# Two feed-forward units moved into the last expert slot, and the weight splits spread over fifteen units

## The chip, the cores and the metric

The kernel runs on one core of a Trainium2 chip. The metric is the device time of one execution, in microseconds (us). Engines are named as the profile names them: PE (TensorE, matrix products), DVE (VectorE), ACT (ScalarE), POOL (GpSimd) and SP (SyncE, which here only issues DMAs). Each engine works through its own instructions in order; semaphores make one engine wait for another.

## The reference

Three layers over 2304 tokens of width 512, all in float32:

```
scores = mask(q @ k.T / 8); attn = softmax(scores) @ v        # 4 x 8 heads, 576 tokens, blocks of 64
e = argmax(xn @ en.T / tau); x = gate * (relu(x @ w1[e]) @ w2[e])   # 8 experts, 512 -> 1024 -> 512
h = x @ w_in                                                   # feed-forward: 512 -> 2048
g = (a0 + a1 h + a2 h^2 + a3 h^3) / (1 + |b0||h| + |b1| h^2 + 1e-6)
out = g @ w_out                                                # 2048 -> 512
```

The change concerns the last layer and its border with the experts.

## The kernel before, in words

Attention comes first, then the experts, then the feed-forward layer. The experts work on slots of 128 tokens that go to the same expert: 23 slots here, and a conditional block (`tc.If(live > COMMON)`, L1219) would do further ones; in these runs it is skipped, but every engine has to reach it and step over it. A slot gathers its tokens, turns them (L783), multiplies by w1 (L816), applies relu (L824), turns the result (L831; L839 and L840 copy it to SBUF, L845 makes its remainder), multiplies by w2 (L861), scales by the gate (ACT, `ys`, L874) and scatters to `x2_d` (POOL, L875). HEAD, PLAN1 and FOOT are strings that write out the order of these steps; FOOT has the last slots, 20 to 22.

Products keep float32 accuracy by splitting every operand into a rounded part and a remainder: `hi` is a copy rounded to the PE's format, `lo` is the operand minus `hi`, and a product is three matmuls (hi x hi, hi x lo, lo x hi).

The feed-forward layer has 96 **units**: six token blocks J of 384 tokens, times 16 slices f of 128 hidden columns. A unit has 12 matmuls into a PSUM tile `mp` (`hidden`, L1273), a chain of elementwise steps that forms g, and 9 matmuls that add g @ w_out to three accumulators (`project`, L1349). The chain, by the letters that the plan string UNIT uses: S, A, U (ACT: the square, |b0 h| and a2 + a3 h, L1283 to L1291), q (DVE: the denominator, L1303), d and e (DVE: the numerator, L1295 and L1299, the last readers of `mp`), R and Q (ACT: reciprocal root and its square, L1307 and L1312), E (DVE, L1316), r (ACT, L1320), f (DVE, L1324), g (DVE, L1328), h (DVE: `gh`, the rounded g, L1332) and l (POOL: `gl`, the remainder, L1337). R needs another table on ACT than the steps ahead of it, so the first R is led by a table load.

UNIT interleaves units: a letter with a digit n in period t works on unit t - n. So in period t PE does the products of unit t (H0) and then the projection of unit t - 3 (P3); DVE does E of unit t - 1, h of t - 2, q and d of t, f of t - 1, e of t and g of t - 1. `mp` has two buffers, so H of unit t waits for step e of unit t - 2.

Weights of the feed-forward layer arrive coded and are decoded during the expert phase. The tiles of the first PRE = 4 slices f are split there at once (hi on ACT, L217, lo on POOL, L218) and kept; the other 24 are stored to `w_d` and come back during the first feed-forward units (`load_w`, L1249; four staging tiles `wst`). There `split_w` makes hi (L1261, on DVE) and lo (L1264, DVE and POOL by turns). Period t of the first 20 uses the plan FIRST, with two such splits each.

At the end `deliver` copies the three accumulators to SBUF (L1364, L1366) and POOL sends them (L1372).

Of the kernel before, what the change touches and what calls it, by code (L numbers as in the profile page):

```python
# [29 lines left out]
PRE = 4  # L30
# [17 lines left out]
FOOT = "C00.20 C01.20 L10.19 D C02.20 T0.19 L11.19 R10.20 T1.19 AH.19 C03.20 AL0.19 G.22 X.21 XH.21 XL.21 H00.21 C10.19 L00.21 C11.19 D C12.19 C13.19 R11.20 H01.21 L02.21 RL.20 L01.21 R00.22 L03.21 D R01.22 T0.20 D H10.20 Y.19 L10.20 L11.20 T1.20 C00.21 C01.21 R10.21 D C02.21 AH.20 AL0.20 X.22 XH.22 C03.21 H00.22 L01.22 C10.20 L00.22 XL.22 C11.20 H01.22 RL.21 C12.20 C13.20 R11.21 D L02.22 H10.21 C00.22 L03.22 C01.22 T0.21 L11.21 D L10.21 Y.20 T1.21 AH.21 AL0.21 R10.22 D C02.22 C03.22 C10.21 C11.21 C12.21 RL.22 C13.21 R11.22 T0.22 H10.22 Y.21 D L10.22 L11.22 T1.22 AH.22 D AL0.22 D C10.22 C11.22 C12.22 D D C13.22 Y.22 D"  # L48
# [7 lines left out]
def block_attn_moe_moe2(ctx: ExitStack, tc, ap):  # L56
# [1169 lines left out]
    with ExitStack() as c3:  # L1226
        wt_b = c3.enter_context(tc.tile_pool(name="wt_b", bufs=1, side="right"))
        st_p = c3.enter_context(tc.tile_pool(name="st", bufs=NST))
        x2_p.append(c3.enter_context(tc.tile_pool(name="x2b", bufs=1)))
        g_p = c3.enter_context(tc.tile_pool(name="g", bufs=2))  # L1230
        ps_a = c3.enter_context(tc.tile_pool(name="ps_a", bufs=NA, space=PSUM))
# [35 lines left out]
        def hidden(i):  # L1267
            J, f = seq[i]
            xh, xl = x2_t[J]
            hp = ps_m.tile([128, TN], F32, name="mp", tag="mp")  # L1270
            for k in range(4):
                for n, (ww, xx) in enumerate(((wih, xh), (wil, xh), (wih, xl))):
                    nc.tensor.matmul(  # L1273
                        out=hp, lhsT=ww[f][:, k], rhs=xx[:, k], start=(k == 0 and n == 0), stop=(k == 3 and n == 2))
            if f == 15:
# [3 lines left out]
        def h_sq(i):
            hp, y, sq, t, q, g = e_t[i]
            nc.scalar.activation(out=sq, in_=hp, func=ACTF.Square)  # L1283

        def h_abs(i):
            hp, y, sq, t, q, g = e_t[i]
            nc.scalar.activation(out=q, in_=hp, func=ACTF.Abs, scale=ab[:, 4:5])  # L1287

        def h_top(i):
            hp, y, sq, t, q, g = e_t[i]  # L1290
            nc.scalar.activation(out=t, in_=hp, func=ACTF.Identity, scale=ab[:, 3:4], bias=ab[:, 2:3])  # L1291

        def p_two(i):
            hp, y, sq, t, q, g = e_t[i]
            nc.vector.tensor_tensor(out=t, in0=t, in1=hp, op=ALU.mult)  # L1295
# [12 lines left out]

        def q_inv(i):
            hp, y, sq, t, q, g = e_t[i]  # L1310
            y = e_t[i][1] = ps_z.tile([128, TN], F32, name="zp", tag="zp")
            nc.scalar.activation(out=y, in_=g, func=ACTF.Square)  # L1312

        def q_err(i):
            hp, y, sq, t, q, g = e_t[i]
            nc.vector.scalar_tensor_tensor(out=q, in0=q, scalar=ONE6, in1=y, op0=ALU.add, op1=ALU.mult)  # L1316

        def e_sq(i):
            hp, y, sq, t, q, g = e_t[i]
            nc.scalar.activation(out=q, in_=q, func=ACTF.Square, scale=-1.0, bias=three2)  # L1320

        def y_fix(i):
            hp, y, sq, t, q, g = e_t[i]
            nc.vector.scalar_tensor_tensor(out=y, in0=q, scalar=0.75, in1=y, op0=ALU.add, op1=ALU.mult)  # L1324

        def g_mul(i):
            hp, y, sq, t, q, g = e_t[i]
            nc.vector.scalar_tensor_tensor(out=g, in0=t, scalar=ab[:, 0:1], in1=y, op0=ALU.add, op1=ALU.mult)  # L1328

        def g_hi(i):  # L1330
            g_t[i] = [g_p.tile([128, TN], F32R, name=n, tag=n, bufs=NG) for n in ("gh", "gl")]
            nc.vector.tensor_copy(g_t[i][0], e_t[i][5])  # L1332

        def g_lo(i):
            gh, gl = g_t[i]
            eng = nc.vector if i == len(seq) - 1 else nc.gpsimd
            eng.tensor_tensor(out=gl, in0=e_t.pop(i)[5], in1=gh.bitcast(F32), op=ALU.subtract)  # L1337

        def project(i):
# [5 lines left out]
            if i == len(seq) - 1:  # L1345
                parts = [(t, n) for ns in ((0, 1), (2,)) for t in range(3) for n in ns]
# [34 lines left out]
        def next_x2(i):  # L1381
# [65 lines left out]
```

## Time and profile before

| what | us |
|---|---|
| median of 3 runs (lowest, highest) | 991.58 (984.66, 993.79) |
| the profiled execution | 985.55 |
| its span, first to last instruction | 983.5 |
| busy in the span: PE, DVE, ACT, POOL | 926.5, 790.2, 684.6, 288.4 |
| mean granted PE clock | 0.987 of full speed |

The profiled execution is 6.03 us under the median of the runs and 2.05 us longer than its own span. Times in rows count from the start of the span. A busy PE hides every other engine, so the places to look at are those where PE is idle or its granted clock is below 1. The feed-forward layer begins at 546.55 us.

### The profile page before, as it was taken

To read this page: it belongs to the slowest core of one execution; us is meant where nothing else is said; L and a number is where in the kernel's file an instruction comes from. 1 tells how busy PE (TensorE), PEld (TensorE's weight loads), DVE (VectorE), ACT (ScalarE), POOL (GpSimd) and SP (SyncE) were. 2 spreads that over 40 slices of the span, in tenths; PEclk is the share of its full clock that TensorE was granted. 3 is DMA by queue.
4 is the path that set the end of the run, shared out by engine and by line. 5 is a ranking of instruction groups with operands and counts; after the bars stand their busy time and mean duration, and the time that the engine had idled before them with its cause. 6 is when DMAs were issued, how large, how long until landed. Compare 5 with 4: busy or idle time off the path is not lost. (4 is left out here: it accounts for less than half of the span.)

```text
span 983.5 us, 15433 instructions
## 1 busy us (share of the span) xinstructions
PE 926.5 (94%) x5120; PEld 740.1 (75%) x5120; DVE 790.2 (80%) x1484; ACT 684.6 (70%) x1380; POOL 288.4 (29%) x266
## 2 busy tenths in 40 slices
PE   6999999879889999999999788999999999999995
PEld 5777777664566777777776576889999999999994
DVE  5778788846687786988874599898988898988884
ACT  6777878653665676877765566777777777777773
POOL 4333333201112211333321255232232322322322
PEclk9999999989999999999999999999999999999998
DMA  8227161821267458557324342000101001000000
GB/s 254 70 91 218 59 203 50 299 69 44 79 214 255 177 192 295 172 205 251 129 77 149 108 132 61 33 33 1 35 31 33 22 12 33 33 1 1 33 1 32
DMA packets 43984, 103.00 MB, mean 105 GB/s; under 512 B 6006, under 2 KB 7158, under 8 KB 43904
## 3 DMA queue, kind: packets, MB, share of 16 engines
q1 hardware_dynamic: 38784, 86.54, 27.0%
q0 software_dynamic: 5120, 15.47, 4.4%
q8 instruction: 41, 0.67, 0.3%
q14 instruction: 39, 0.32, 0.1%
HBM read 140.27 MB, written 21.76 MB: 165 GB/s over the span
## 5 line engine op out<-in xcount | busy, mean ns | idle before, releaser
L1337 POOL TENSOR_TENSOR gl<-g,gh 128x384 fp32r<-128x384 f32 x95 | 106.0, 1116 | 247.1 <-DVE gh L1332 218.2
L1273 PE MATMUL mp<-x2h,wih 128*128 128x384 f32 x384 | 130.0, 338 | 5.9 <-DVE t L1299 4.8
L1273 PE MATMUL mp<-x2l,wih 128*128 128x384 f32 x384 | 130.0, 339 | 0.0
L1273 PE MATMUL mp<-x2h,wil 128*128 128x384 f32 x384 | 129.3, 337 | 0.0
L1349 PE MATMUL acc<-woh,gl 128*128 128x512 f32 x288 | 114.9, 400 | 5.9 <-POOL gl L1337 5.9
L769 DVE TENSOR_TENSOR wl<-w0r,wh 128x1024 fp32r<-128x1024 f32 x84 | 98.9, 1221 | 23.8 <-ACT wh L763 22.7
L1349 PE MATMUL acc<-woh,gh 128*128 128x512 f32 x288 | 115.0, 399 | 0.1
L1349 PE MATMUL acc<-wol,gh 128*128 128x512 f32 x288 | 113.7, 395 | 0.0
L1303 DVE SCALAR_TENSOR_TENSOR q<-sq,absb,q 128x384 f32<-128x384 f32 x96 | 83.5, 869 | 31.2 <-ACT q L1287 30.7
L816 PE MATMUL hp<-wh,x 128*128 128x512 f32 x336 | 103.8, 431 | 0.2 <-ACT wh L763 0.2
L1283 ACT ACTIVATE sq<-mp 128x384 f32<-128x384 f32 x96 | 47.0, 489 | 78.5 <-PE mp L1273 75.7
L763 ACT ACTIVATE wh<-w0r 128x2048 fp32r<-128x2048 f32 x42 | 79.5, 1909 | 9.8 <-DMA w0r<-in_moe_w 7.4
L342 ACT ACTIVATE p<-s,nm 128x128 f32<-128x128 f32 (+2 forms) x144 | 78.4, 555 | 11.4 <-DVE nm L355 6.2
L875 POOL DMA_INDIRECT x_d<-ys,sct_i x23 | 35.3, 1537 | 167.5 <-ACT ys L874 155.6
L861 PE MATMUL yp<-w1r,hf 128*128 128x512 f32 x184 | 83.4, 592 | 0.0
L393 ACT ACTIVATE pt<-tp 128x128 f32<-128x128 f32 (+2 forms) x144 | 54.2, 423 | 39.7 <-PE tp L431 26.2
L1273 PEld LDWEIGHTS mp<-x2h,wih 128*128 128x128 f32 x384 | 72.3, 188 | 11.6 <-DVE t L1299 5.9
L816 PEld LDWEIGHTS hp<-wh,x 128*128 128x128 f32 x336 | 61.2, 192 | 19.2 <-issue 8.9
L1273 PEld LDWEIGHTS mp<-x2h,wil 128*128 128x128 f32 x384 | 72.3, 188 | 3.8
L1273 PEld LDWEIGHTS mp<-x2l,wih 128*128 128x128 f32 x384 | 72.3, 188 | 0.0
L1349 PEld LDWEIGHTS acc<-woh,gl 128*128 128x128 f32 x288 | 54.1, 188 | 22.6 <-POOL gl L1337 11.3
L1307 ACT ACTIVATE g<-q,one 128x384 f32<-128x384 f32 x96 | 59.5, 620 | 16.3 <-DVE q L1303 15.4
(304 smaller groups left out, 2252.7 us busy)
## 6 DMA issues: line engine op xcount, KB each, us to landing
w0r<-in_moe_w SPq DMA_DIRECT2D x44, 1024.0 KB
w1r<-in_moe_w SPq DMA_DIRECT2D x44, 1024.0 KB
w<-in_moe_w_in SPq DMA_DIRECT2D x16, 512.0 KB
w<-in_moe_w_out SPq DMA_DIRECT2D x16, 512.0 KB
w_d<-dm SPq DMA_DIRECT2D x24, 256.0 KB
wst<-w_d SPq DMA_DIRECT2D x24, 256.0 KB
kr<-in_k SPq DMA_DIRECT2D x16, 288.0 KB
xr<-x_d SPq DMA_DIRECT2D x6, 768.0 KB
```

Of the source, the lines that this page charges most:

```text
L342: nc.scalar.activation(out=pt, in_=src, func=ACTF.Exp, bias=bi, accum_out=pair_t[n][3][:, c, hh:hh + 1])
L393: nc.scalar.activation(out=o, in_=i, func=ACTF.Copy)
L763: nc.scalar.activation(out=out, in_=src, func=ACTF.Copy)
L769: eng.tensor_tensor(out=wl, in0=w_raw[m][k][:, j], in1=wh_t[s, m, k][:, j].bitcast(F32), op=ALU.subtract)
L816: nc.tensor.matmul(out=hp[:, n], lhsT=xx[:, ks], rhs=ww[:, 512 * n:512 * n + 512], start=(c == 0 and j == 0), stop=(c == 3 and j == len(pa ...
L861: nc.tensor.matmul(out=yp, lhsT=xx[:, 128 * f:128 * f + 128], rhs=ww[:, 512 * j:512 * j + 512], start=(c == 0 and q == 0 and j == 0), stop ...
L1273: nc.tensor.matmul(out=hp, lhsT=ww[f][:, k], rhs=xx[:, k], start=(k == 0 and n == 0), stop=(k == 3 and n == 2))
L1283: nc.scalar.activation(out=sq, in_=hp, func=ACTF.Square)
L1303: nc.vector.scalar_tensor_tensor(out=q, in0=sq, scalar=absb[:, 1:2], in1=q, op0=ALU.mult, op1=ALU.add)
L1307: nc.scalar.activation(out=g, in_=q, func=ACTF.Abs_reciprocal_sqrt, bias=one6)
L1337: eng.tensor_tensor(out=gl, in0=e_t.pop(i)[5], in1=gh.bitcast(F32), op=ALU.subtract)
L1349: nc.tensor.matmul(out=acc[J][t], lhsT=gg[:, 128 * t:128 * t + 128], rhs=ww[f], start=(f == 0 and n == 0), stop=(f == 15 and n == 2))
```

## The change

- The first HOIST = 2 units (all steps but the projection) run in FOOT, inside slot 22, ahead of the conditional block. Their products go to PSUM tiles of the expert pools, and their chains work in the staging tile of w1 (`w_raw`), which slot 22 has used up by then; gh and gl go to a pool of their own (`gx`).
- PRE is 5: ten decoded tiles are split and kept in the expert phase, not eight. 22 tiles remain to be brought back.
- The splits are spread over periods 2 to 16, one in even and two in odd periods. hi is made on ACT instead of DVE; lo of a w_in tile is made on DVE, lo of a w_out tile on POOL. LATE = 4 orders a slice's w_out tile four places behind its w_in tile.
- One plan serves all periods; the splits stand at its end (i0 behind Q0, o0 behind g1).
- The pools of the feed-forward layer wait for the tiles whose memory they reuse (`reuse_waits="tile"`), not for the pools as wholes.
- The last unit's nine projection matmuls finish the accumulators one by one.

```diff
-PRE = 4
+PRE = 5
...
-LATE = 2
-ON = 20
+LATE = 4
+HOIST = 2
+SPLITS = range(2, 17)
...
-HI = 'vvv'
-LO = 'vp'
...
-FIRST = 'H0 i0 O0 S0 E1 A0 h2 q0 U0 r1 X0 P3 d0 R0 f1 o0 e0 Q0 l2 g1 i0 o0'
-UNIT = 'H0 s1 O0 S0 E1 A0 h2 q0 U0 r1 X0 P3 d0 R0 f1 e0 Q0 l2 g1'
-LAST = UNIT
+UNIT = 'H0 s1 O0 S0 E1 A0 h2 q0 U0 r1 X0 P3 d0 R0 f1 e0 Q0 i0 l2 g1 o0'
...
+    def h_tile(i):
+        if i == 0:
+            return pool["ps_x"].tile([128, 512], F32, name="xp", tag="xp")[:, 0:TN]
+        if i < HOIST:
+            return pool["ps_h"].tile([128, 2, 512], F32, name="hp", tag="hp")[:, 0, 0:TN]
+        return ff["m"].tile([128, TN], F32, name="mp", tag="mp")
...
+        if i < HOIST:
+            raw = w_raw[0][i].rearrange("p a f -> p (a f)")
+            e_t[i] = [hp, raw[:, 4 * TN:5 * TN]] + [raw[:, TN * n:TN * n + TN] for n in range(4)]
...
-        ps_m = c3.enter_context(tc.tile_pool(name="ps_m", bufs=NM, space=PSUM))
+        ff["m"] = c3.enter_context(tc.tile_pool(name="ps_m", bufs=NM, space=PSUM, reuse_waits="tile"))
...
             if kind == "i":
-                if HI[n % len(HI)] == "a":
-                    nc.scalar.activation(out=hi, in_=st_t[n], func=ACTF.Copy)
-                else:
-                    nc.vector.tensor_copy(hi, st_t[n])
+                nc.scalar.activation(out=hi, in_=st_t[n], func=ACTF.Copy)
             else:
-                eng = nc.gpsimd if LO[n % len(LO)] == "p" else nc.vector
+                eng = nc.vector if late[n] < 16 else nc.gpsimd
...
-                parts = [(t, n) for ns in ((0, 1), (2,)) for t in range(3) for n in ns]
+                parts = [(0, 0), (0, 1), (1, 0), (0, 2), (1, 1), (1, 2), (2, 0), (2, 1), (2, 2)]
...
-        due = dict.fromkeys(unit, 0)
+        due = dict.fromkeys(unit, HOIST)
+        due["P"] = 0
...
-            t = 0
+            t = HOIST
...
-                        split_w(name)
+                        for _ in range((1 + t % 2) * (t in SPLITS)):
+                            split_w(name)
```

The FOOT string of the change is that of before with the hoisted steps written in, as `uH.0` for step H of unit 0. What this makes of ACT's order inside slot 22 shows in two pieces, first before, from the last relu to the conditional block (`wh` and `ys` are the slot's weight copy and output, `hh` and `hf` its turned relu):

```order
L824 ACTIVATE hs<-hp 128x1024
L763 ACTIVATE wh<-w1r_144 128x2048
L874 ACTIVATE ys<-yp,gate_s 128x512
L839 ACTIVATE hh<-tp 128x512
L840 ACTIVATE hf<-tp 128x512
L874 ACTIVATE ys<-yp,gate_s 128x512
L1218 TENSOR_LOAD enc_i
```

And the same place in the change (`w0r_142` and `w0r_143` are the scratch of units 0 and 1):

```order
L871 ACTIVATE ys<-yp,gate_s 128x512
L1144 ACTIVATE w0r_142<-xp 128x384
L1148 ACTIVATE w0r_142<-xp,ab 128x384
L1152 ACTIVATE w0r_142<-xp,ab 128x384
L836 ACTIVATE hh<-tp 128x512
L837 ACTIVATE hf<-tp 128x512
L1168 ACT_TABLE_LOAD
...
L1174 ACTIVATE w0r_143<-w0r_143 128x384
L1182 ACTIVATE w0r_143<-w0r_143,three_105 128x384
L871 ACTIVATE ys<-yp,gate_s 128x512
```

Unit 0's first three steps now stand ahead of slot 22's `hh`, and the slot's last `ys` stands behind step r of unit 1.

The second place is DVE in one of the first feed-forward periods. Before, from E to E:

```order
L1316 SCALAR_TENSOR_TENSOR q<-q,zp 128x384
L1332 CAST gh<-g 128x384
L1303 SCALAR_TENSOR_TENSOR q<-sq,absb,q 128x384
L1295 TENSOR_TENSOR t<-t,mp 128x384
L1324 SCALAR_TENSOR_TENSOR zp<-q,zp 128x384
L1264 TENSOR_TENSOR wil_6209<-wst,wih_6208 128x512
L1299 SCALAR_TENSOR_TENSOR t<-t,ab,mp 128x384
L1328 SCALAR_TENSOR_TENSOR g<-t,ab,zp 128x384
L1261 CAST woh_6202<-wst 128x512
L1261 CAST wih_6212<-wst 128x512
```

In the change:

```order
L1178 SCALAR_TENSOR_TENSOR q<-q,zp 128x384
L1196 CAST gh<-g 128x384
L1164 SCALAR_TENSOR_TENSOR q<-sq,absb,q 128x384
L1156 TENSOR_TENSOR t<-t,mp 128x384
L1186 SCALAR_TENSOR_TENSOR zp<-q,zp 128x384
L1160 SCALAR_TENSOR_TENSOR t<-t,ab,mp 128x384
L1190 SCALAR_TENSOR_TENSOR g<-t,ab,zp 128x384
L1355 TENSOR_TENSOR wil_6280<-wst,wih_6279 128x512
```

The two casts have left DVE, and the one subtraction has moved behind g.

## Rows read from the trace of the kernel before

**Rows 1.** The page's first line.

```profile
span 983.5 us, 15433 instructions
```

**Rows 2.** Windows: stretch, length, then busy us (instructions) of PE, PEld, DVE, ACT, POOL; clock, DMA.

```profile
553.75:559.30 5.55, 3.49 (x18) 3.17 (x19) 5.55 (x12) 4.14 (x8) 1.54 (x2) 1.00 0.47 119
559.30:562.70 3.40, 3.40 (x11) 2.62 (x10) 3.40 (x8) 2.05 (x5) 2.40 (x2) 0.52 0.39 119
562.70:620.00 57.30, 50.99 (x245) 41.91 (x244) 57.23 (x113) 36.56 (x72) 27.57 (x21) 1.00 0.31 88
620.00:960.00 340.00, 340.00 (x1728) 307.80 (x1728) 299.80 (x581) 256.73 (x506) 103.47 (x95) 1.00 0.06 22
```

**Rows 3.** The chain that ended last: start, us, what; PE's pieces in the steady stretch.

```profile
616.86 2.11 PE mp L1273 x12
618.96 0.33 PE zp L1111 x3
619.29 2.08 PE acc L1349 x9
```

**Rows 4.** Timeline, border of experts and feed-forward: start, us, engine, line, [idle before <-releaser].

```profile
536.10 1.04 PE L831 MATMUL tp<-ident,hs 128*128 128x128 f32 x8
539.40 0.74 PE L861 MATMUL yp<-wh,hl 128*128 128x512 f32 x2 [0.85 <-DVE hl L845]
545.53 0.69 ACT L874 ACTIVATE ys<-yp,gate_s 128x512 f32<-128x512 f32 x1 [7.28 <-PE yp L861]
546.53 26.84 SPq L1249 DMA_DIRECT2D wst<-w_d  x13
546.55 0.44 PE L1273 MATMUL mp<-x2h,wih 128*128 128x384 f32 x1 [1.06 <-ACTq L1219]
...
550.61 1.28 ACT L1307 ACT_TABLE_LOAD   x1
551.15 0.43 DVE L1261 CAST wih<-wst 128x512 fp32r<-128x512 f32 x1 [11.80 <-DMA wst<-w_d]
552.14 0.61 ACT L1307 ACTIVATE g<-q,one 128x384 f32<-128x384 f32 x1 [0.24 <-DVE q L1303]
553.75 0.44 PE L1273 MATMUL mp<-x2h,wih 128*128 128x384 f32 x1 [2.76 <-DVE t L1299]
554.74 1.31 DVE L1303 SCALAR_TENSOR_TENSOR q<-sq,absb,q 128x384 f32<-128x384 f32 x1
```

**Rows 5.** Timeline of DVE and POOL inside one of the first twenty periods.

```profile
567.20 0.68 DVE L1264 TENSOR_TENSOR wil<-wst,wih 128x512 fp32r<-128x512 f32 x1
...
569.34 1.40 POOL L1264 TENSOR_TENSOR wol<-wst,woh 128x512 fp32r<-128x512 f32 x1 [2.13 <-DVE woh L1261]
569.98 0.98 DVE L1332 CAST gh<-g 128x384 fp32r<-128x384 f32 x1
```

**Rows 6.** Timeline of DVE in the steady stretch, from one E to the next.

```profile
709.02 0.54 DVE L1316 SCALAR_TENSOR_TENSOR q<-q,zp 128x384 f32<-128x384 f32 x1
...
712.26 0.55 DVE L1316 SCALAR_TENSOR_TENSOR q<-q,zp 128x384 f32<-128x384 f32 x1
712.73 0.35 DVE L1332 CAST gh<-g 128x384 fp32r<-128x384 f32 x1
```

**Rows 7.** Line L217: ACT's rounding of a kept weight tile; ns least/median/most.

```profile
L217 ACT ACTIVATE wih<-dm x4: 610/629/632, 407.6 to 485.7; 128x512 fp32r<-128x512 f32 x4
```

**Rows 8.** Timeline, the last unit: its S, R and r on ACT, its projection, the output copy.

```profile
963.83 0.49 ACT L1283 ACTIVATE sq<-mp 128x384 f32<-128x384 f32 x1 [0.58 <-PE mp L1273]
965.74 0.62 ACT L1307 ACTIVATE g<-q,one 128x384 f32<-128x384 f32 x1
967.99 0.62 ACT L1320 ACTIVATE q<-q,three 128x384 f32<-128x384 f32 x1 [1.11 <-DVE q L1316]
...
971.85 0.39 PE L1349 MATMUL acc<-wol,gh 128*128 128x512 f32 x1
...
972.96 1.08 ACT L1366 ACTIVATE ot<-acc 128x512 f32<-128x512 f32 x2 [4.35 <-PE acc L1349]
```

More of the change, by code (lines that the diff above doesn't have):

```diff
@@ L1113, in turn_x2, with hidden @@
         nc.vector.tensor_tensor(out=xl[:, k], in0=tp, in1=xh.bitcast(F32)[:, k], op=ALU.subtract)
+    seq = [(J, f) for J in range(NJ) for f in range(16)]
+    e_t, g_t, ff = {}, {}, {}
+    def h_tile(i):
[4 more added lines that the diff above has]
+        return ff["m"].tile([128, TN], F32, name="mp", tag="mp")
+    def hidden(i):
+        J, f = seq[i]
+        xh, xl = x2_t[J]
+        hp = h_tile(i)
+        for k in range(4):
+            for n, (ww, xx) in enumerate(((wih, xh), (wil, xh), (wih, xl))):
+                nc.tensor.matmul(
+                    out=hp, lhsT=ww[f][:, k], rhs=xx[:, k], start=(k == 0 and n == 0), stop=(k == 3 and n == 2))
+        if f == 15:
+            x2_t.pop(J)
+        if i < HOIST:
+            raw = w_raw[0][i].rearrange("p a f -> p (a f)")
+            e_t[i] = [hp, raw[:, 4 * TN:5 * TN]] + [raw[:, TN * n:TN * n + TN] for n in range(4)]
+        else:
+            e_t[i] = [hp, None] + [ff["g"].tile([128, TN], F32, name=n, tag=n, bufs=b) for n, b in GB]
@@ new lines, in h_sq, with h_abs, h_top, p_two @@
+    def h_sq(i):
+        hp, y, sq, t, q, g = e_t[i]
+        nc.scalar.activation(out=sq, in_=hp, func=ACTF.Square)
+    def h_abs(i):
+        hp, y, sq, t, q, g = e_t[i]
+        nc.scalar.activation(out=q, in_=hp, func=ACTF.Abs, scale=ab[:, 4:5])
+    def h_top(i):
+        hp, y, sq, t, q, g = e_t[i]
+        nc.scalar.activation(out=t, in_=hp, func=ACTF.Identity, scale=ab[:, 3:4], bias=ab[:, 2:3])
+    def p_two(i):
+        hp, y, sq, t, q, g = e_t[i]
+        nc.vector.tensor_tensor(out=t, in0=t, in1=hp, op=ALU.mult)
@@ new lines, in p_three, with q_sum, q_root, q_inv @@
+    def p_three(i):
+        hp, y, sq, t, q, g = e_t[i]
+        nc.vector.scalar_tensor_tensor(out=t, in0=t, scalar=ab[:, 1:2], in1=hp, op0=ALU.add, op1=ALU.mult)
+    def q_sum(i):
+        hp, y, sq, t, q, g = e_t[i]
+        nc.vector.scalar_tensor_tensor(out=q, in0=sq, scalar=absb[:, 1:2], in1=q, op0=ALU.mult, op1=ALU.add)
+    def q_root(i):
+        hp, y, sq, t, q, g = e_t[i]
+        nc.scalar.activation(out=g, in_=q, func=ACTF.Abs_reciprocal_sqrt, bias=one6)
+    def q_inv(i):
+        hp, y, sq, t, q, g = e_t[i]
+        if i >= HOIST:
+            y = e_t[i][1] = ff["z"].tile([128, TN], F32, name="zp", tag="zp")
+        nc.scalar.activation(out=y, in_=g, func=ACTF.Square)
@@ new lines, in q_err, with e_sq, y_fix, g_mul @@
+    def q_err(i):
+        hp, y, sq, t, q, g = e_t[i]
+        nc.vector.scalar_tensor_tensor(out=q, in0=q, scalar=ONE6, in1=y, op0=ALU.add, op1=ALU.mult)
+    def e_sq(i):
+        hp, y, sq, t, q, g = e_t[i]
+        nc.scalar.activation(out=q, in_=q, func=ACTF.Square, scale=-1.0, bias=three2)
+    def y_fix(i):
+        hp, y, sq, t, q, g = e_t[i]
+        nc.vector.scalar_tensor_tensor(out=y, in0=q, scalar=0.75, in1=y, op0=ALU.add, op1=ALU.mult)
+    def g_mul(i):
+        hp, y, sq, t, q, g = e_t[i]
+        nc.vector.scalar_tensor_tensor(out=g, in0=t, scalar=ab[:, 0:1], in1=y, op0=ALU.add, op1=ALU.mult)
@@ new lines, in g_hi, with g_lo @@
+    def g_hi(i):
+        g_t[i] = [
+            ff["gx" if i % NG < HOIST else "g"].tile([128, TN], F32R, name=n, tag=n, bufs=HOIST if i % NG < HOIST else NG - HOIST)
+            for n in ("gh", "gl")]
+        nc.vector.tensor_copy(g_t[i][0], e_t[i][5])
+    def g_lo(i):
+        gh, gl = g_t[i]
+        eng = nc.vector if i == len(seq) - 1 else nc.gpsimd
+        eng.tensor_tensor(out=gl, in0=e_t.pop(i)[5], in1=gh.bitcast(F32), op=ALU.subtract)
+    unit = {
+        "H": hidden, "S": h_sq, "A": h_abs, "U": h_top, "d": p_two, "e": p_three, "q": q_sum, "R": q_root, "Q": q_inv,
+        "E": q_err, "r": e_sq, "f": y_fix, "g": g_mul, "h": g_hi, "l": g_lo}
@@ L1147, in block_attn_moe_moe2 @@
             slot_ops[f"C{m}{c}"] = partial(mm, c=c)
+    for name, op in unit.items():
+        slot_ops["u" + name] = op
     plan1 = [(w[:-1], int(w[-1])) for w in PLAN1.split()]
@@ L1226, in block_attn_moe_moe2 @@
     with ExitStack() as c3:
[L1227 to L1231, printed above, removed]
-        ps_m = c3.enter_context(tc.tile_pool(name="ps_m", bufs=NM, space=PSUM))
-        ps_z = c3.enter_context(tc.tile_pool(name="ps_z", bufs=8 - NA - NM, space=PSUM))
+        wt_b = c3.enter_context(tc.tile_pool(name="wt_b", bufs=1, side="right", reuse_waits="tile"))
+        st_p = c3.enter_context(tc.tile_pool(name="st", bufs=NST, reuse_waits="tile"))
+        x2_p.append(c3.enter_context(tc.tile_pool(name="x2b", bufs=1, reuse_waits="tile")))
+        ff["g"] = c3.enter_context(tc.tile_pool(name="g", bufs=2, reuse_waits="tile"))
+        ps_a = c3.enter_context(tc.tile_pool(name="ps_a", bufs=NA, space=PSUM, reuse_waits="tile"))
+        ff["m"] = c3.enter_context(tc.tile_pool(name="ps_m", bufs=NM, space=PSUM, reuse_waits="tile"))
+        ps_z = ff["z"] = c3.enter_context(tc.tile_pool(name="ps_z", bufs=8 - NA - NM, space=PSUM, reuse_waits="tile"))
         w_tiles(wt_b, range(PRE, 16))
-        st_t, e_t, g_t, acc = {}, {}, {}, {}
+        st_t, acc = {}, {}
         turn_ps = lambda: ps_z.tile([128, TN], F32, name="zp", tag="zp")
-        seq = [(J, f) for J in range(NJ) for f in range(16)]
         late = []
@@ L1265, in split_w @@
                 load_w(n + NST)
[L1267 to L1277, printed above, removed]
@@ L1281, in h_sq @@
[L1281 to L1295, printed above, removed]
@@ L1309, in q_inv @@
[L1309 to L1337, printed above, removed]
         def project(i):
@@ L1386, in next_x2 @@
                 turn_x2(J + 1, X2.index(f) - 1)
-        unit = {
-            "H": hidden, "S": h_sq, "A": h_abs, "U": h_top, "d": p_two, "e": p_three, "q": q_sum, "R": q_root, "Q": q_inv,
-            "E": q_err, "r": e_sq, "f": y_fix, "g": g_mul, "h": g_hi, "l": g_lo, "P": project, "X": next_x2}
-        due = dict.fromkeys(unit, 0)
-        plans = [[(w[0], int(w[1])) for w in p.split()] for p in (FIRST, UNIT, LAST)]
+        unit.update(P=project, X=next_x2)
+        due = dict.fromkeys(unit, HOIST)
+        due["P"] = 0
+        plan = [(w[0], int(w[1])) for w in UNIT.split()]
         with tc.manual_schedule():
@@ L1395, in block_attn_moe_moe2 @@
                 load_w(n)
-            t = 0
+            t = HOIST
             while due["P"] < len(seq):
-                for name, d in plans[(t >= ON) + (t >= len(seq) - 16)]:
+                for name, d in plan:
                     if name == "s":
```

12 lines of the change are left out of this document (2 added, 10 removed).

## The prediction, as it went on record

> **What bounds the kernel now.** I read the 40 slices first, then windows around every slice in which PE is not full, then the timeline inside them. From 620 to 960 us PE is busy for all of 340 us [rows 2]: a unit costs it 2.11 for the products and 2.08 for the projection, 4.19 in all [rows 3], and no other engine matters there. So the change can move the end only at the border and in the first periods. At the border PE waits 1.06 for ACT to step over the conditional block and, after two units, 2.76 for DVE's step e [rows 4]. Behind that it is idle for 5.55 - 3.49 = 2.06 and for 57.30 - 50.99 = 6.31 [rows 2], together 8.37, while DVE is busy for 62.78 of the 62.85 us of the same two stretches: the first periods are bound by DVE. [...]
>
> **(a) The hoisted units.** I follow slot 22 in the change's order. PE's turning of the slot began at 536.10 [rows 4]; the products of unit 0 now stand there, and the turning follows at 538.2, the products of unit 1 at 539.2 to 541.3 (2.11 and 1.04 each). Before, PE stood still in that place, 0.85 of it ahead of 539.40 [rows 4], so a good part of the 4.2 us is filled in. The slot's second product, 539.40 to 545.53 before, now starts its `hl` part at about 541.7 and ends at 547.9.
> The chains set the rest. S of unit 0 starts 0.2 behind its products, at 538.4. S to R of the last unit takes 1.91 [rows 8], 0.5 of it another unit's r, so ACT is through S, A and U at 539.8; `hh` and `hf` (two copies of the size of rows 7, overlapping to about 1.1) and the table load of 1.28 [rows 4] put R at 542.2. From R to the end of r the last unit takes 968.61 - 965.74 = 2.87 [rows 8], of which 0.5 is another unit's g: r of unit 0 ends between 544.5 and 545.1. DVE then needs f, g and h, about 1.5, before q of unit 1; 0.65 for q, and again 2.4 to 2.9 to the end of its r: 549.0 to 550.1. Slot 22's `ys` stands behind that r on ACT, and PE may start unit 2 only when ACT has stepped over the block, 546.55 - 545.53 = 1.02 after the start of `ys` [rows 4]. Unit 2 starts at **550.0**, where before it started at 553.75: 3.75 gained. Bounds: if `ys` waited for PE alone, 548.9 (4.85 gained); with every link late, 551.4 (2.35).
> Behind the waiting ACT nothing else is late: POOL's two `gl` end about 1.1 after unit 1's gh, ahead of S of unit 2, which they must precede. The table load was paid at 550.61 before and now delays the chain in slot 22. The row shows R at 552.14, 0.25 behind the load's end and released by DVE [rows 4], so no more than 0.25 was left over. [...]
>
> **(b) The first periods.** Before, a period asked of DVE 3.24 [E to E, rows 6], a wil of 0.60 (the 0.68 of rows 5 less overlap), two casts of 0.34 (0.43 in rows 4 less overlap), and 0.63 by which gh is longer beside POOL's wol: 0.98 against 0.35 [rows 5, 6]. That is 5.15, against 4.19 on PE. Now the casts are gone. Over periods 2 to 16: 15 x 3.24 = 48.6, 11 wil x 0.60 = 6.6, 11 gh beside a wol x 0.63 = 6.9, four x2l (each with a turn on PE of 0.33 [rows 3]) x 0.47 = 1.9: 64.0. PE needs 15 x 4.19 + 4 x 0.33 = 64.2. So DVE keeps pace on the average, but not in odd periods, which have two splits: 4.47 there. The slack is about 1.5, since a projection comes three periods behind its products, and in periods 7 and 11 wil is late by up to 0.8, because woh stands ahead of wih on ACT and wol is already on POOL. ACT has 256.73 / 340 x 4.19 = 3.16 a period [rows 2], in all 47.5, and 22 roundings at 0.55 to 0.63 [rows 7], 12.1 to 13.9: at most 61.4 of 64.2, tight and in order. I leave 1.5 of PE's 8.37 idle: 6.87 gained. Bounds: nothing left (8.37), 4 left (4.4).
> Loads: the first still lands before it is asked for; the next three wait for DVE to step over the block, about 550.8, and take up to 551.15 - 546.53 = 4.6 [rows 4], 555.4; wih6 is rounded at about 559. Two tiles fewer come back. Their two kept splits fall in the expert phase, under a PE that is full there, and cost nothing; without that cover they would cost two roundings of 0.63 [rows 7].
>
> **(c) The clock.** PE's holes shrink to one of about 2 us ahead of unit 2. I take no fall: 1.63 gained. Bounds: 0 (the same fall) to 1.63.
>
> **(d) The end.** The first accumulator was released with the seventh of the last nine matmuls, the copy starting at 972.96; now it takes the fourth, which starts at 971.85 and not three steps of 0.23 later [rows 8]. POOL's three sends follow one another, so the end moves with the first: 0.68 gained, bounds 0 and 0.7.
>
> **Sum.** 3.75 + 6.87 + 1.63 + 0.68 = 12.9 off 985.55, the profiled execution (span 983.5 [rows 1] and 2.05 around it): 972.6. The median of the runs is 6.03 above that execution, for a reason the profile does not show; carried over, 991.58 - 12.9 = **978.6**.
>
> **Rivals.**
> *Half of it.* The splits are chained ACT, DVE, ACT in order: a rounding that waits for its load, or runs late, holds S of the next unit. If a period costs 4.6 on the average, PE idles 15 x 0.32 = 4.8 less 1.5 of slack, and with chains at their late end and the clock falling once more the gain is 2.35 + 5.0 + 0 + 0.5 = 7.9: 983.7. For it: ACT at 61 of 64. Against: DVE had its casts in the same place before and waited for a load only once [rows 4]. Chance 0.23.
> *Slower: DVE beside POOL.* DVE's q took 1.31 at 554.74 [rows 4], and gh 0.98, where POOL was subtracting. [...] If now every period's q is held (0.70 more than the 0.61 that I take for it), every gh (0.63) and every wil (0.8), DVE needs 48.6 + 6.6 + 1.9 + 10.5 + 9.5 + 8.8 = 85.9 for the fifteen, and PE idles 85.9 - 64.2 - 1.5 = 20.2, 11.8 more than before; with (a) and (d) gained and the clock as before that is 7.4 slower: 999. It turns slower from 5.2 a period. Against: when DVE runs without a pause its q follows gh at once and is ahead of POOL's gl. Chance 0.05.
> *Nothing arrives.* The border's gain is given back by a later hole, or the runs' spread of 9 us covers it: 988. Chance 0.10.
> *The forecast*, 0.62.
>
> **Numbers.** A measurement of this kernel tells about 1%, 9.9 us, from no change. The forecast and its bounds give gains of 7 to 15.6, mostly above 10: 0.60 of faster there, and a little from the other cases. Half of it and nothing arriving fall within 1%. Range: low end 985.55 - 15.6 = 970, on the profiled execution's level with all upper bounds; high end 991.58 - 5.5 = 986, beyond the half case.
>
> **What would show it.** Right: PE starts unit 2 near 550 with `ys` just behind a step r; between there and 620 PE idles less than 3; DVE is no longer full there; no clock of 0.5; the first output copy starts three matmuls earlier. Wrong: unit 2 past 551.5, periods of 4.5 and more on PE with DVE or ACT as releasers, q of 1.2 in each, or S waiting behind a rounding that waits for a load.

## The result: 977.0 us, 1.2% faster

| kernel | median us (lowest, highest; runs) | ratio to before, 95% interval | profiled execution | its span |
|---|---|---|---|---|
| before | 989.07 (984.66, 993.79; 4) | | 985.55 | 983.5 |
| the change | 977.02 (973.93, 979.49; 4) | 0.9877 (0.9838 to 0.9916) | 973.93 | 971.0 |

Before's runs are the three shown above and a fourth that was made beside the change. The span fell by 12.5 us [rows 1]. The first lines of the page after:

```profile
span 971.0 us, 15430 instructions
PE 922.9 (95%) x5120; PEld 741.4 (76%) x5120; DVE 781.4 (80%) x1459; ACT 696.0 (72%) x1404; POOL 292.2 (30%) x267
```

The border after, by the timeline (columns as in rows 4; `w0r` is the scratch of the hoisted units, `ys` slot 22's output):

```profile
535.41 0.74 PE L1130 MATMUL xp<-x2h,wih 128*128 128x384 f32 x1
538.10 0.49 ACT L1144 ACTIVATE w0r<-xp 128x384 f32<-128x384 f32 x1 [1.40 <-PE xp L1130]
540.61 1.28 ACT L1168 ACT_TABLE_LOAD   x1
541.91 0.62 ACT L1168 ACTIVATE w0r<-w0r,one 128x384 f32<-128x384 f32 x1
548.32 0.61 ACT L1182 ACTIVATE w0r<-w0r,three 128x384 f32<-128x384 f32 x1 [0.62 <-DVE w0r L1178]
548.84 0.67 ACT L871 ACTIVATE ys<-yp,gate_s 128x512 f32<-128x512 f32 x1
549.61 0.44 PE L1130 MATMUL mp<-x2h,wih 128*128 128x384 f32 x1 [2.23 <-ACTq L1314]
```

`ys` stands right behind unit 1's step r, and unit 2 starts 0.77 behind the start of `ys`, as ACT has stepped over the block: 549.61, against 553.75 before [rows 4].

The first periods, in windows (columns as in rows 2):

```profile
550.00:620.00 70.00, 66.78 (x331) 59.19 (x330) 62.71 (x119) 58.81 (x115) 31.63 (x26) 0.98 0.33 103
590.00:595.00 5.00, 3.40 (x17) 2.62 (x15) 4.74 (x11) 4.38 (x10) 2.42 (x2) 1.00 0.20 54
595.00:600.00 5.00, 4.85 (x16) 4.13 (x17) 5.00 (x10) 2.95 (x6) 2.56 (x3) 0.66 0.36 107
605.00:610.00 5.00, 4.19 (x22) 3.54 (x21) 4.58 (x9) 4.04 (x9) 3.29 (x3) 1.00 0.46 141
615.00:620.00 5.00, 4.35 (x22) 3.90 (x22) 5.00 (x8) 3.59 (x7) 4.00 (x4) 1.00 0.00 0
```

Of 70 us PE is idle for 3.22, all of it in the four short windows, and none from 550 to 590; DVE is no longer full. In one window the granted clock is 0.66, which costs 0.34 x 5 = 1.70. Where PE waits shows in its timeline:

```profile
593.80 0.50 PE L1368 MATMUL acc<-woh,gh 128*128 128x512 f32 x1 [0.90 <-ACT woh L1352]
595.15 0.50 PE L1368 MATMUL acc<-wol,gh 128*128 128x512 f32 x1 [0.85 <-POOL wol L1355]
606.48 0.50 PE L1368 MATMUL acc<-wol,gh 128*128 128x512 f32 x1 [0.81 <-POOL wol L1355]
615.74 0.51 PE L1368 MATMUL acc<-wol,gh 128*128 128x512 f32 x1 [0.65 <-POOL wol L1355]
```

All four are waits for a w_out tile that is still being split, by the projections of units 9, 11 and 13. With LATE = 4 the tiles of these slices are the second split of periods 11, 13 and 15, and the projection wants them in the next period.

The end (answers to rows 8): S of the last unit, and the first copy.

```profile
951.99 0.49 ACT L1144 ACTIVATE sq<-mp 128x384 f32<-128x384 f32 x1 [0.59 <-PE mp L1130]
958.67 0.56 DVE L1201 TENSOR_TENSOR gl<-g,gh 128x384 fp32r<-128x384 f32 x1
960.45 0.60 ACT L1385 ACTIVATE ot<-acc 128x512 f32<-128x512 f32 x1 [3.67 <-PE acc L1368]
```

**The span in pieces.** What lies ahead of the change's first instruction differs from run to run by 10 us (last section), so kernels are compared from a common point, 3.03 behind the start of the eight matmuls that end slot 21's second product. Those eight before, then in the change, with the second matmul of unit 0:

```profile
532.66 3.59 PE L861 MATMUL yp<-w1r,hf 128*128 128x512 f32 x8
```

```profile
532.38 3.59 PE L858 MATMUL yp<-w1r,hf 128*128 128x512 f32 x8
535.99 0.34 PE L1130 MATMUL xp<-x2h,wil 128*128 128x384 f32 x1
```

In the change the point is 535.41, where the record of unit 0's first matmul starts; before it is 535.69. The start of PE's next instruction is not the same point in both: before it is 536.10 [rows 4], 3.44 behind the start of the eight, while the record of unit 0's first matmul starts 0.41 sooner, and the next matmul follows only 0.58 behind it, where 0.17 is usual. "Border" is from the common point to the start of unit 2, "middle" from there to S of the last unit, "end" from there to the span's end. Before: 18.06 + 410.08 + 19.67 = 447.81. After: 14.20 + 402.38 + 19.01 = 435.59. So 3.86 came from the border, 7.70 from the middle, 0.66 from the end, and 0.28 from ahead of all that: 12.5.

### The profile page after: what moved, and what is told of

The parts are those of the page before. It is cut to its first block, busy times and chain, and to the rows that moved or that the text cites. A ratio compares the mean times of both kernels' runs of the same rounds, so it can differ in the third digit from the quotient of the medians.

```text
span 971.0 us, 15430 instructions
## 1 busy us (share of the span) xinstructions
PE 922.9 (95%) x5120; PEld 741.4 (76%) x5120; DVE 781.4 (80%) x1459; ACT 696.0 (72%) x1404; POOL 292.2 (30%) x267
## 5 line engine op out<-in xcount | busy, mean ns | idle before, releaser
L1201 POOL TENSOR_TENSOR gl<-g,gh 128x384 fp32r<-128x384 f32 x93 | 103.6, 1114 | 252.1 <-DVE gh L1196 230.9
L1130 PE MATMUL mp<-x2h,wih 128*128 128x384 f32 x376 | 127.0, 338 | 2.2 <-ACTq L1314 2.2
L1130 PE MATMUL mp<-x2l,wih 128*128 128x384 f32 x376 | 127.1, 338 | 0.0
L766 DVE TENSOR_TENSOR wl<-w0r,wh 128x1024 fp32r<-128x1024 f32 x84 | 108.1, 1337 | 23.1 <-ACT wh L760 21.8
L1130 PE MATMUL mp<-x2h,wil 128*128 128x384 f32 x376 | 126.6, 337 | 0.0
L872 POOL DMA_INDIRECT x_d<-ys,sct_i x23 | 30.3, 1316 | 168.5 <-ACT ys L871 165.8
L813 PEld LDWEIGHTS hp<-wh,x 128*128 128x128 f32 x336 | 61.3, 192 | 19.2 <-issue 7.6
```

Of the source, the lines that this page charges most:

```text
L766: eng.tensor_tensor(out=wl, in0=w_raw[m][k][:, j], in1=wh_t[s, m, k][:, j].bitcast(F32), op=ALU.subtract)
L813: nc.tensor.matmul(out=hp[:, n], lhsT=xx[:, ks], rhs=ww[:, 512 * n:512 * n + 512], start=(c == 0 and j == 0), stop=(c == 3 and j == len(pa ...
L1130: nc.tensor.matmul(out=hp, lhsT=ww[f][:, k], rhs=xx[:, k], start=(k == 0 and n == 0), stop=(k == 3 and n == 2))
```

## The experiments

| kernel | median us | ratio to before | border | middle | end | sum |
|---|---|---|---|---|---|---|
| before | 989.07 | | 18.06 | 410.08 | 19.67 | 447.81 |
| the change | 977.02 | 0.9877 | 14.20 | 402.38 | 19.01 | 435.59 |
| not hoisted | 974.81 | 0.9875 | 15.89 | 404.62 | 18.99 | 439.50 |
| old splits | 978.32 | 0.9881 | 14.21 | 406.27 | 19.76 | 440.24 |
| rounded on DVE | 984.52 | 0.9935 | 14.21 | 407.66 | 19.79 | 441.66 |
| LATE = 2 | 979.76 | 0.9910 | 14.20 | 407.83 | 21.28 | 443.31 |
| LATE = 3 | 974.22 | 0.9865 | 14.21 | 400.95 | 19.82 | 434.98 |
| LATE = 3, ahead | 972.63 | 0.9847 | 14.19 | 399.03 | 19.81 | 433.03 |
| remainders on DVE | 975.44 | 0.9872 | 14.20 | 401.62 | 19.80 | 435.62 |
| pools as wholes | 981.88 | 0.9926 | 15.84 | 403.78 | 19.77 | 439.39 |
| old end | 978.94 | 0.9899 | 14.20 | 402.35 | 20.43 | 436.98 |
| ahead, ys early | 969.68 | 0.9835 | 13.69 | 399.16 | 19.81 | 432.66 |
| that, remainders on DVE | 973.24 | 0.9841 | 13.68 | 398.46 | 19.79 | 431.93 |
| that, end on DVE | 970.57 | 0.9837 | 13.69 | 398.41 | 19.47 | 431.57 |

The ratios' intervals reach 0.003 to 0.005 to each side, so medians tell these kernels apart only at the extremes; the pieces are of one profiled execution each. How well pieces repeat shows in the change and the kernel with the old end, which do the same up to the last unit: border and middle together are 416.58 and 416.55. Each ratio is to runs of before made beside that kernel. An end of 19.8 instead of 19.0 has a reason of its own (last section) and is left out of the readings; in that of 21.28 the clock falls as well: from 962.61 to 965.59 matmuls of the last projections start 0.43 apart, not 0.23.

**Not hoisted.**

```diff
-HOIST = 2
+HOIST = 0
...
```

The hoisted steps leave FOOT with it.

> The change without its hoisted units: units 0 and 1 run behind the conditional block again, all else as in the change. Theory (the border's gain comes from hoisting): PE begins unit 2 near 553 instead of 549.6, some 3.5 us later (2.5 to 4.5), and from there on the two traces agree within 1 us; the time is about 3.5 above the change. Rival (what was gained at the border comes from pools that wait for tiles instead of whole pools): PE begins unit 2 before 551, and the time is within 1 us of the change.

The sum is 3.9 longer, within what the theory had, but not where it had it. (By medians nothing of it shows: 974.81 against 977.02.) Unit 2 starts only 1.69 later than in the change (15.89 against 14.20 behind the common point). The rival's sign, unit 2 before 551, came only because this execution was at the common point 2.11 earlier than the change's. PE's timeline shows the other hole ahead of unit 3:

```profile
549.19 0.44 PE L1130 MATMUL mp<-x2h,wih 128*128 128x384 f32 x1 [0.82 <-DVE t L1160]
553.46 0.44 PE L1130 MATMUL mp<-x2h,wih 128*128 128x384 f32 x1 [1.91 <-DVE t L1160]
```

The first of these was 2.76 before [rows 4]. There DVE stood in front of a rounding whose load had not landed, until 551.15, and unit 0's q behind it; with no split in the first periods q runs at once:

```profile
547.37 0.62 DVE L1164 SCALAR_TENSOR_TENSOR q<-sq,absb,q 128x384 f32<-128x384 f32 x1 [10.65 <-ACT q L1148]
```

So of the 3.86 at the border 2.17 come without any hoisting, mostly from splits that no longer stand in the first two periods. The hoisting brings the other 1.69 and the next 2.24, the middle's difference.

**Old splits.** Two in every early period, hi on DVE, lo by turns, the old order of tiles; hoisting and the fifth kept pair stay.

```diff
-LATE = 4
-SPLITS = range(2, 17)
+LATE = 2
+ON = 20
+FIRST = 'H0 i0 O0 S0 E1 A0 h2 q0 U0 r1 X0 P3 d0 R0 f1 o0 e0 Q0 l2 g1 i0 o0'
...
-                nc.scalar.activation(out=hi, in_=st_t[n], func=ACTF.Copy)
+                nc.vector.tensor_copy(hi, st_t[n])
```

> The change with the splits as before: two in each of the first periods, rounding on DVE, lo by turns on DVE and POOL, the old order of tiles; hoisting and five kept tiles stay. Theory (DVE's pace set the first periods): 11 periods at 5.15 against 4.19 on PE make 10.6 of idle PE less some 1.5 of slack, about 9, against the 3.2 that the change leaves; the time is 5 to 8 us above the change, and DVE is busy all through 553 to 605. Rival (hoisting took away what the first periods lost, since PE's chain now runs ahead): PE idles 3 to 4 there as in the change, and the time is within 2 us of it.

DVE is full again and PE waits for gl in nearly every early period, as before. One window and one wait of this kernel:

```profile
575.00:580.00 5.00, 4.34 (x22) 3.48 (x22) 5.00 (x11) 3.17 (x6) 2.41 (x3) 1.00 0.78 262
576.10 0.50 PE L1370 MATMUL acc<-woh,gl 128*128 128x512 f32 x1 [0.66 <-POOL gl L1203]
```

The mechanism is the theory's, the size is smaller: the middle is 3.89 longer, not 5 to 8. The clock reads 1.00 in every window from 540 to 630, so the 1.70 that the change loses to it are not lost here; without that it would be 5.6. The fifth kept pair is the one part of the change that no run undoes. This kernel keeps it, and hoisting, and its middle is 3.81 under before's; 1.63 of that is the fall of the clock that before has [rows 2], and how hoisting and the pair share the rest is not shown.

**Rounded on DVE**, the spread kept.

```diff
-                nc.scalar.activation(out=hi, in_=st_t[n], func=ACTF.Copy)
+                nc.vector.tensor_copy(hi, st_t[n])
```

> The change with the rounding back on DVE, the spread over fifteen periods kept. Theory (both the spread and the move to ScalarE count): DVE then has 64.0 + 22 x 0.34 = 71.5 us of work for PE's 64.2, PE idles 71.5 - 64.2 - 1.5 = 5.8 between units 2 and 17, 2.6 more than in the change. Rival 1 (the spread alone did it): no more than 1 above the change. Rival 2 (ScalarE was the late one in the change, holding the w_out tiles back): PE's waits for wol shrink, and the time is 1 to 3 us below the change.

The middle is 5.28 longer. Both rivals are out: the spread without the move to ScalarE is no better than the old plan (1.39 longer than with the old splits, but the clock reads 0.66 in one window of 5 us here and never falls there, which is 1.70). My 2.6 counted DVE's sum alone; what it leaves out is that the tiles themselves come later:

```profile
604.66 0.50 PE L1368 MATMUL acc<-woh,gh 128*128 128x512 f32 x1 [2.08 <-DVE woh L1352]
606.12 0.80 PE L1368 MATMUL acc<-wol,gh 128*128 128x512 f32 x1 [0.96 <-POOL wol L1355]
```

**What is left idle: LATE = 2.**

```diff
-LATE = 4
+LATE = 2
```

> The change with a slice's w_out tile two places behind its w_in tile instead of four (LATE = 2): the w_out tiles of slices 9 to 12 are split two periods ahead of their projection instead of one. Theory (what is left idle in the first periods is PE waiting for w_out tiles that are split too late): the waits of 0.90, 0.85, 0.81 and 0.65 for woh and wol near 594, 595, 606 and 616 go, with them the fall of the clock near 597 (1.70), and the time is 3 to 5 us below the change. Rival 1 (DVE's pace leaves the idle time): the waits move to other tiles and the time stays within 1 us. Rival 2 (now the w_in tiles of slices 14 and 15 are late): PE waits for wil of these about as long, 1 to 3 us, and the time is 0 to 2 below the change.

My theory's forecast failed: the waits for w_out tiles go, all but one of 0.38, and worse ones for w_in tiles come. The middle is 5.45 longer, far more than rival 2 had; 1.70 of it is a second fall of the clock. Unit 15 shows why:

```profile
600.45 0.52 PE L1130 MATMUL mp<-x2h,wih 128*128 128x384 f32 x1 [2.69 <-ACT wih L1352]
604.75 0.49 ACT L1144 ACTIVATE sq<-mp 128x384 f32<-128x384 f32 x1 [3.84 <-PE mp L1130]
607.70 0.49 ACT L1174 ACTIVATE zp<-g 128x384 f32<-128x384 f32 x1
608.13 0.61 ACT L1352 ACTIVATE wih<-wst 128x512 fp32r<-128x512 f32 x1
608.79 0.44 PE L1130 MATMUL mp<-x2h,wih 128*128 128x384 f32 x1 [1.65 <-ACT wih L1352]
```

Slice 15's w_in tile is now rounded in period 14, behind step Q of unit 14, and unit 15 wants it at the start of the next period. So products, S, q, R, Q, rounding and the next products form one chain from unit to unit: 600.45 to 608.79 is 8.34 us for a period that PE does in 4.19, of which the low clock makes 1.70. A late w_out tile costs PE what is left of its split; a late w_in tile puts the whole latency of the chain into the period. The clock reads 0.66 in two windows of 5 us here.

**LATE = 3**, the compromise.

```diff
-LATE = 4
+LATE = 3
```

> The change with LATE = 3: the w_out tile of slice 9 is split in period 10 instead of 11, those of slices 11 and 13 stand first in their period instead of second, and no w_in tile is split later than two periods ahead of its unit. Measured on PE from the end of slot 21's second product to the span's end, since what lies ahead moves with the clock (the change: 435.6; LATE = 2: 443.3). Theory (the second split of an odd period comes too late for a tile that is wanted in the next period, whichever tile it is): the waits of 0.90, 0.85, 0.81 and 0.65 shrink to under 1 together, the clock does not fall, and this stretch is 2 to 4 us shorter, 432 to 433.5. Rival (the order of tiles only passes the lateness on): 435 to 438, with waits for wih or wil in place of those for wol.

Border and middle are 1.4 shorter than in the change, between theory and rival. The clock does not fall (1.00 from 548 to 620), which is the gain (1.70); but the waits add up to 3.03, in other places (0.86 and 0.55 for wol, 0.53 for wil, 0.67 for x2l, 0.23 for gl, 0.19 for woh). So the order of tiles alone mostly passes the lateness on.

**LATE = 3, one split earlier.**

```diff
-                        for _ in range((1 + t % 2) * (t in SPLITS)):
+                        for _ in range((1 + (t % 2 or t == 6)) * (t in SPLITS)):
```

> LATE = 3, and two splits in period 6 instead of one, so that every later tile is split one place earlier. Theory (lateness of single tiles is all that is left): no wait of PE for a weight tile, 432 from the end of slot 21's second product to the span's end, the same as or 0.5 below LATE = 3 alone. Rival (ACT and DVE have no room for three periods of two splits in a row): PE waits for gl or S around periods 6 to 8, 0.5 to 1.5 us, and the stretch is 433 to 435.

Border and middle are 413.22, 3.36 below the change, 1.70 of it from a clock that does not fall (1.00 from 548 to 620), and PE waits for no weight tile. The rival's waits for gl do come (0.23, 0.18, 0.51, 0.32), but the gain stands. This settles what left PE idle in the change: single tiles split too late, not DVE's or ACT's pace.

**Remainders on DVE**, none on POOL, the change otherwise.

```diff
-                eng = nc.vector if late[n] < 16 else nc.gpsimd
+                eng = nc.vector
```

> The change with all remainders of tiles on DVE, none on POOL (order of tiles as in the change). Theory (DVE's instructions are stretched while POOL subtracts, so moving the subtraction from POOL to DVE is nearly free for DVE): gh in periods 3 to 16 falls from 0.635 to about 0.4, DVE's work for the fifteen periods is 48.6 + 22 x 0.60 + 1.9 = 63.7 as before, and the wol that PE waits for come 0.6 earlier each: from the end of slot 21's second product to the span's end 434 to 435.5, against 435.6. Rival (DVE is the bound and 11 more subtractions of 0.6 to 0.78 are added to it): PE idles 6.6 to 8.6 more, less 1.5 of slack: 440 to 443.

Eleven subtractions more cost DVE nothing that PE feels: the middle is 0.76 shorter, and the rival's 440 to 443 is out. The theory's 434 to 435.5 is missed by 0.1, with the longer end in it. The groups of DVE's instructions from 552 to 620, first of this kernel, then of the change (count, then busy us and mean ns):

```profile
L1355 DVE TENSOR_TENSOR wil<-wst,wih 128x512 fp32r<-128x512 f32 x11 | 7.5, 685 | 0.7 <-ACT wih L1352 0.7
L1196 DVE CAST gh<-g 128x384 fp32r<-128x384 f32 x13 | 4.6, 351 | 0.0
```

```profile
L1196 DVE CAST gh<-g 128x384 fp32r<-128x384 f32 x14 | 8.9, 635 | 0.0
L1355 DVE TENSOR_TENSOR wil<-wst,wih 128x512 fp32r<-128x512 f32 x11 | 8.5, 778 | 1.0 <-ACT wih L1352 1.0
```

In the change six of the 14 gh take 0.97 to 1.09, and two of the wil 1.00 and 1.37; each of them runs beside a subtraction of a weight tile on POOL. In this kernel, with none there, no gh takes more than 0.36 and no wil more than 0.70.

**Pools as wholes.** The feed-forward pools without `reuse_waits="tile"`.

> The change with the feed-forward pools waiting for whole pools again, not for single tiles. Theory (it is worth little, since unit 2 waits for ACT to step over the conditional block anyway): from the end of slot 21's second product to the span's end within 0.5 of the change's 435.6. Rival (the first loads of coded tiles and the first scratch tiles then wait for slot 22's last readers, unit 1's chain and the scatter among them): the first loads land some 1 to 2 us later, the first splits hold ACT, and the stretch is 1 to 3 us longer.

The theory is wrong, and the rival's size is right: 3.8 longer, 3.0 without the end. But its path, late loads, is there only in part. PE now waits for DVE, which steps over the block behind unit 1's g and h; by the records S of unit 2 does wait for a load, but PE then has no wait until 603:

```profile
557.55 0.66 PE L1130 MATMUL mp<-x2h,wih 128*128 128x384 f32 x1 [3.86 <-DVEq L1314]
561.55 0.49 ACT L1144 ACTIVATE sq<-mp 128x384 f32<-128x384 f32 x1 [5.74 <-DMA wst<-w_d]
```

Unit 2 is 1.64 later, and after this longer hole the clock falls at the border (0.74 and 0.92 in two windows of 5 us, 1.70) and once more near 607 (from 606.82 matmuls start 0.43 apart, not 0.23), one fall more than in the change, which makes the middle 1.40 longer. The small edit to the pools is what lets the hoisted chains run on behind the start of unit 2.

**Old end.**

```diff
-                parts = [(0, 0), (0, 1), (1, 0), (0, 2), (1, 1), (1, 2), (2, 0), (2, 1), (2, 2)]
+                parts = [(t, n) for ns in ((0, 1), (2,)) for t in range(3) for n in ns]
```

> The change with the last unit's nine projection matmuls in the old order. From the start of the last gl on DVE to the span's end the kernel before took 13.0 us and the change 12.3. Theory (the first accumulator's copy sets the three sends): 13.0, so 0.65 longer, with everything ahead of it as in the change. Rival (the end is set by the last accumulator or by POOL's own pace): 12.3 to 12.5.

The last gl starts at 962.81 and the span ends at 975.8: 12.99, as the theory has it.

**Toward a better kernel.** `ys` ahead of unit 1's r, on top of LATE = 3 and the earlier split; then all remainders on DVE; then gl of the third last unit on DVE.

```diff
-... C11.22 ur.1 uf.1 ug.1 C12.22 D D C13.22 uh.1 ul.1 Y.22 D D D
+... C11.22 C12.22 D D C13.22 Y.22 ur.1 uf.1 ug.1 uh.1 ul.1 D D D
...
-        eng = nc.vector if i == len(seq) - 1 else nc.gpsimd
+        eng = nc.vector if i in (len(seq) - 3, len(seq) - 1) else nc.gpsimd
```

> LATE = 3 with two splits in period 6 (433.0 us from the end of slot 21's second product to the span's end), and slot 22's last ys placed ahead of step r of unit 1 on ACT. Theory (ACT steps over the conditional block 0.77 after the start of whichever of the two is last; r of unit 1 can start 0.5 before ys does now): PE starts unit 2 at 13.7 instead of 14.2 after that point, and the stretch is 432.5. Rival (unit 1's f and g come later on DVE, or the clock falls after the hole): unit 2 at 13.7, but 433 or more to the end.

> The same with all remainders of tiles on DVE. Theory (with two splits in a period wil on DVE takes 1.36 to 1.42 beside POOL's wol against 0.68 alone, so the pair costs DVE as much as two subtractions of its own, and POOL's gl comes late behind wol): PE's four waits for gl (0.23, 0.18, 0.51, 0.32) go or shrink to under 0.4 together; 431.5 to 432 to the end. Rival (DVE has 11 more subtractions in order, which delay E and so r and g): PE waits for gh or gl of 0.3 or more in the odd periods, 433 to 435.

> The same again, with gl of the third last unit on DVE, not POOL, so that the last unit's q on DVE (1.47 in the runs where POOL's gl had started 0.04 us earlier or less, 0.62 in those where q was first) has nothing beside it. [...] Rival (the added gl on DVE costs what q gains): 19.8 or more.

Each forecast held in its size: the border 13.69, the sum 432.66; then a middle 0.70 shorter and a sum of 431.93; then an end of 19.47 (19.2 to 19.6 expected). The second theory's path held only in part: a wait of 0.58 for gl is left, where it had under 0.4 for all, and one of 0.42 for x2l. The last kernel's sum is 4.0 us under the change, and its ratio to before 0.9837 (0.9796 to 0.9878); that of the first of the three is 0.9835 (0.9798 to 0.9872). Against the change's 0.9877 the intervals overlap, so the medians alone don't prove it; the pieces show where it comes from.

## Why the prediction was right, and where it was not

The time was forecast at 978.6 and is 977.02; the sum of gains was 12.9, the span's is 12.5. The forecast's case is the one that came; that its terms (b) and (c) come so near is in part luck, as errors of 3.4 and 2.6 in them stand against each other.

- **(a), 3.75, measured 3.86.** The chain came out link by link: R at 541.91 (forecast 542.2, with the whole phase 0.28 earlier), the end of unit 1's r at 548.93 (549.0 to 550.1), unit 2 at 549.61 (550.0). What it gave to hoisting alone is three things: hoisting (1.69), splits that left the first two periods (most of the 2.17 that come without it), and pools that wait for tiles (1.64 lost without them), to which the prediction gave no term.
- **The table load.** The forecast had R right behind it, and R starts 0.02 behind the load's end (540.61 + 1.28 = 541.89).
- **(b), 6.87, and (c), 1.63: 8.50 together, measured 7.70.** (c) is the low clock of before, (1 - 0.52) x 3.40 [rows 2]. Two steps failed. The 1.5 us left idle were 3.22, and not by "odd periods" that outrun DVE's slack, but by w_out tiles that are wanted one period behind their split; I had worked out lateness in periods 7 and 11 only, from ACT's order, and not asked for each tile in which period it is split and in which it is wanted. And "I take no fall" of the clock was wrong: it fell for 1.70 behind the holes near 594. Against that, the stretch before held more than I read. The windows showed 8.37 idle and 1.63 of clock, 10.0; but it became 7.70 shorter with 3.22 + 1.70 = 4.92 still lost by the same reading, so it held about 12.6. The ends of matmuls in the records are modelled, and the starts show what that hides. One of PE's waits before:

```profile
571.36 0.40 PE L1349 MATMUL acc<-wol,gh 128*128 128x512 f32 x1
572.41 0.50 PE L1349 MATMUL acc<-woh,gl 128*128 128x512 f32 x1 [0.66 <-POOL gl L1337]
572.75 0.40 PE L1349 MATMUL acc<-woh,gh 128*128 128x512 f32 x1
```

Starts here are usually 0.23 apart. The second is 0.82 late and the third 0.11 more, 0.93 in all for an idle time of 0.66. Before has 12 such waits in the middle, the change 4: counted by starts they cost 11.6 and 4.4, by idle time 8.37 and 3.22. Over all matmuls of the middle, what the starts lie further apart than the median of their kind adds up to 17.45 before and 9.74 after, 7.7 apart.

- **(d), 0.68, measured 0.66**, and 0.66 again when undone.
- **DVE's sum.** 64.0 for fifteen periods: the change's DVE is busy for 62.71 of 70, with gh at 0.635 and wil at 0.778. The gh that ran beside a subtraction of a weight tile on POOL took 0.97 to 1.09, against 0.36 at most in the kernel that has none of these there (remainders on DVE). The sum had 11 gh stretched by 0.63, where six were. The slower rival, with every q, gh and wil stretched, had no room, as DVE still had 7.29 us of pauses in those 70.
- **"Half of it"** needed ACT to be the limit; ACT is busy for 58.81 of 70. Its guess on the clock, one more fall, was the right one.
- **The level of the runs**, taken over as 6.03 with no reason, has one: the clock ahead of the layer, 0.97 to 0.99 in the first 530 us (last section).

## What to carry to other kernels

When work is spread over periods, write down for every item the period and the place in it where it is made, and where it is wanted; a balanced sum per engine says nothing of that. Of two kinds of late items, keep early those that feed the head of the chain that makes the next one: their lateness costs the chain's latency, not the remainder of one instruction. And undo each part by itself: parts that look small (how a pool waits) may be what the large one stands on.

## What the runs showed of the chip

- **The spread of the runs is the clock.** The fourteen profiled executions reach the common point between 533.1 and 543.1 us, in code that is the same but for the fifth kept pair of tiles. The eight that are there by 536.5 have a mean granted clock of 0.99 in the first 530 us, the six that come at 538.5 or later 0.98 or 0.97. Among the 13 runs of before that were made beside the last kernel, the fastest (984.40) has a mean clock of 0.988 over its span, and the slowest (992.27) 0.982. Windows of the latest (the second but last of the table), then of the change:

```profile
100.00:200.00 100.00, 93.29 (x817) 72.81 (x815) 80.47 (x199) 78.43 (x266) 31.73 (x29) 0.97 0.45 150
200.00:300.00 100.00, 86.54 (x427) 55.82 (x424) 63.56 (x159) 54.03 (x96) 10.51 (x9) 0.93 0.29 99
```

```profile
100.00:200.00 100.00, 93.39 (x841) 72.38 (x838) 82.56 (x204) 79.46 (x271) 31.85 (x29) 1.00 0.45 150
200.00:300.00 100.00, 88.20 (x440) 58.03 (x437) 68.71 (x162) 56.77 (x98) 14.09 (x11) 0.97 0.37 124
```

Here the difference, 0.03 x 100 + 0.04 x 100 = 7, is nearly all of the 7.7 by which the two reach the common point apart.

- **The same hole, with and without a fall.** PE's hole of 2.2 ahead of unit 2 left the clock at 1.00 in seven kernels; in the one with remainders on DVE it fell there, and not at the later hole:

```profile
550.00:555.00 5.00, 2.78 (x12) 2.32 (x11) 2.74 (x6) 1.93 (x4) 1.54 (x3) 0.87 0.01 3
555.00:560.00 5.00, 5.00 (x23) 4.74 (x22) 2.03 (x4) 3.57 (x8) 0.88 (x1) 0.79 0.49 171
```

The falls measured have about the same price: (0.13 + 0.21) x 5 = 1.70 here, 0.34 x 5 in the change and twice in LATE = 2. What decides whether a hole of this size brings one stays open.

- **A few hundredths between two starts on DVE and POOL went with 0.8 us at the end.** In the three kernels with an end of 19.0 or 19.67, before among them, the last unit's q took 0.62, in the others but one about 1.46. The change, and then the kernel with remainders on DVE on top of all else:

```profile
952.99 0.62 DVE L1164 SCALAR_TENSOR_TENSOR q<-sq,absb,q 128x384 f32<-128x384 f32 x1
953.05 1.44 POOL L1201 TENSOR_TENSOR gl<-g,gh 128x384 fp32r<-128x384 f32 x1 [3.30 <-DVE gh L1196]
```

```profile
956.21 1.46 DVE L1164 SCALAR_TENSOR_TENSOR q<-sq,absb,q 128x384 f32<-128x384 f32 x1
956.24 1.02 POOL L1201 TENSOR_TENSOR gl<-g,gh 128x384 fp32r<-128x384 f32 x1 [3.29 <-DVE gh L1196]
```

In each pair one takes no longer than alone, and the other 0.84 (q) or 0.42 (gl) more. By the records q starts first in both, 0.06 and 0.03 ahead, so my expectation had the order wrong. So it is in all: gl is the longer one in the three kernels where it starts 0.06 behind q, and q in the ten where gl starts 0.01 to 0.04 behind it; why, stays open. With that gl on DVE, behind it in order, q takes 0.62 again:

```profile
948.43 0.62 DVE L1164 SCALAR_TENSOR_TENSOR q<-sq,absb,q 128x384 f32<-128x384 f32 x1
950.49 0.55 DVE L1201 TENSOR_TENSOR gl<-g,gh 128x384 fp32r<-128x384 f32 x1
```
